# Planning the order of five instruction queues by the longest path, in a linear-attention and MoE kernel

## The chip, the cores and the metric

One core of a Trainium2 chip runs the whole program. The metric is the device time of one execution in microseconds (us). The core's engines are named as in its profile: PE (matrix products), PEld (its weight loads), DVE (vector), ACT (scalar functions), POOL, and SP, which issues the DMAs (its queue is called SPq). Each takes its instructions from a queue of its own, strictly in order.

## The reference

A recurrent linear attention over 768 steps is followed by two MoE layers (one expert each, so plain two-layer networks). Cut to what is computed:

```python
# r, k, v, w, a, b: (4, 8, 768, 40) float32; w_in: (320, 2048), w_out: (2048, 320)
for t in range(S):                                   # for each batch and head
    y[:, :, t] = np.einsum('bhd,bhde->bhe', rt, state)
    Sa = np.einsum('bhde,bhe->bhd', state, at)
    state = state * wt[:, :, None, :] - np.einsum('bhd,bhe->bhde', Sa, bt) + np.einsum('bhd,bhe->bhde', vt, kt)
x = y.transpose(0, 2, 1, 3).reshape(B * S, H * D)    # (3072, 320)
h = x @ moe_w_in;  x = (h * (1.0 / (1.0 + np.exp(-h)))) @ moe_w_out
h = x @ moe2_w_in; out = (h - np.tanh(h)) @ moe2_w_out
```

## The kernel before

The 768 steps are cut into 12 chunks of 64, and the 32 heads into two halves `hf`. Within a chunk the recurrence is a set of matrix products and one triangular solve; from chunk to chunk only the state is carried. A first stage does, chunk by chunk, the attention and the first MoE layer of the chunk's 256 tokens; a second stage then runs the second MoE layer. Large operands are split into a high and a low fp16 plane, so one product takes several matmuls.

The steps of a chunk, with the tile that each writes and the lines of the trace:

- `load_raw`, `prep` (each half): decay products and fp16 planes on DVE, ACT and POOL, written to `HL`; then 12 DMAs of SP copy `HL` into a slot `LR` (L256), and others write `pd`. `load_v` loads `VU`.
- `p1`, `p2`: the first products, `p1a` (L276) and `p1b` (L296). Readers: `mK` on DVE (L284), `bP` on ACT (L289), `KBt` on ACT (L303).
- `sol_in`, 31 `sol_step`s, `sol_out`: the triangular solve for all heads at once, nearly all on DVE: a transpose (L311), then pairs `tmp` and `Tl` (L321, L323), then two transposes (L333, L334). `mrg1`, `mrg2`: products that merge its blocks, tiles `mg` (L342, L356).
- `ch_x`: `psx` (L370, L372) from the carried state `MT`, and `Xs` from it on ACT (L381). `ch_u`: `psu` (L389), read by L398 and L399, and two copies within `LR` (L401). `ch_s`: the scores `pss` (L409) with `psu2` (L410; the trace calls it psu), read into `Sm` on DVE (L418) and `VU` on ACT (L419). `ch_y`: the output `psy` (L428, L431) and the next state `psm` (L442).
- `ch_ye`: the state is scaled into `Md` on DVE (L453), rounded to `MT` on ACT (L455), its low part goes to `lows` on POOL (L196), and two DMAs copy both into `MT` (L457, L458). The next chunk's `ch_x` of this half needs them: this is the recurrence. `ch_m` transposes the state into `M` (L471, L482 to L484).
- `x_t1`, `x_t2`: the output is transposed (`psyt`, L499), scaled (`pf` on DVE, L510) and split into `xh` and `xl`, input of the MoE layer.
- MoE layer 1, eight hidden tiles `i` a chunk: `mm_h` (`hp`, 16 matmuls, L576 and L577), `act1` (Silu, `gh`, `hs` on ACT at L585 to L587, `gl` on POOL), `mm_o` (`o`, 12 matmuls, L600 to L602). Its weights arrive as float64 bits and are converted once, in 32 pieces (`conv_wi`, `conv_wo`; DVE at L531 and L533, the rest on ACT and POOL), into `wih` and `woh`.

PSUM is shared out so: one bank for `hp`, two for `o`, one for `Tl`, and four that all attention tiles take in turn (`ps_a`, `bufs=4`). `gh` and `gl` have three buffers, `hs`, `xh` and `xl` two.

The order is written by hand. A table `SC` gives each step a due time in eighths of a chunk; `when` puts a step no earlier than what it needs, and the tasks run sorted by time:

```python
at(M0 + i, lambda c=c, i=i: mm_h(1, c, i, w1iv, *x_t[c], ps_h))
...
tasks.sort(key=lambda q: (q[0], q[1]))
for t, _, fn, a in tasks:
    fn(*a)
```

The framework (`TileContext` with `schedule_with_timeline_sim=True`) then schedules the instructions on the engines by its own timeline, following the order of the program. The conversions of the first layer are held back by `gates`, four points in chunk 0.

Of the kernel before, what the change touches and what calls it, by code (L numbers as in the profile page):

```python
# [1 line left out]

# [4 lines left out]

F32 = mybir.dt.float32
F16 = mybir.dt.float16
I32 = mybir.dt.int32  # L10
# [37 lines left out]
def _poly():  # L48
# [19 lines left out]
SC = dict(  # L68
    d=(-0.1673, -0.0563, 0.2069),
    r=(0, 0.3799, 0),  # L70
    dm=(-0.1189, -0.1189, -0.1189),
    raw=(-10.4107, -10.4347),
    prep=(-9.6543, -9.4535),
    v=(-4.211, -3.5903),
    p1=(-10.2371, -9.8163, -9.5719, -9.187),
    p2=(1.1248, 2.0285, 1.4012, 1.5709),
# [9 lines left out]
    x=(-0.9631, -0.0175, 2.3021, 1.3623),  # L86
    xe=0.01,
    u=(0.6994, 1.3329, 1.3307, 2.0705),
# [3 lines left out]
    y=(1.4518, 1.9314, 2.2421, 2.7265),  # L92
    ye=0.0248,
    m=(7.3159, 7.953, 8.873, 8.4506),
# [6 lines left out]
    o=3.2447,  # L101
    c1=(-9.2025, 0.5509, 0.821),
# [1 line left out]
)  # L104


def build(tc, pk, tv, w1i, w1o, w2i, w2o, out, nch=NCH, dbg=None):
# [83 lines left out]
    gates = {}  # L191
    y_t, ps_t, x_t, pf_t = {}, {}, {}, {}
    pd = dram.tile([nch, 2, DM, 2, C], F32, name="pd")

# [21 lines left out]
    def prep(c, hf):  # L216
        w, ra, rkb, rrv = raw_t.pop((c, hf))
        hl = HL
        if c == 0 and hf == 1:
            hl = lr_slot().rearrange("p u n -> p (u n)")[0:120, 0:12 * RW].rearrange("p (j n) -> p j n", j=6)  # L220
            DVE.memset(planes(hl)[0][:, :, 3 * C:LW], 0.0)
        ll, rh, lh, rl = planes(hl)
        k0, v0 = (0, 2 * C) if c % 2 == 0 else (C, 0)

        av, kb, rv, vv = [x.rearrange("p (j t) -> p j t", j=6) for x in (ra, rkb, rrv[:, 0:384], rrv[:, 384:768])]

        pt = at_p.tile([120, 392], F32, tag="pq", name="pq", bufs=1)
# [21 lines left out]
        if c == 0:  # L249
            gates["pool"] = nc.cur_bb.bb.instructions[-1]  # L250
# [8 lines left out]
        if c == 0:  # L259
            gates["sp"] = nc.cur_bb.bb.instructions[-1]  # L260
# [57 lines left out]
    def sol_step(c, j):  # L318
        n, w = 31 - j, j // 2 + 1
        tv_ = tmp[:, 0:n * w].rearrange("p (t s) -> p t s", t=n)  # L320
        DVE.tensor_tensor(tv_, Al[:, j + 1:, j:j + 1].to_broadcast([128, n, w]),  # L321
                          Tl[:, j:j + 1, :w].to_broadcast([128, n, w]), ALU.mult)
        DVE.tensor_tensor(Tl[:, j + 1:, :w], Tl[:, j + 1:, :w], tv_, ALU.add)  # L323
        if c == 0:
            gates["dve"] = nc.cur_bb.bb.instructions[-1]

    def sol_out(c):
        bb = 64 * (c % 2)
# [262 lines left out]
    def mm_o(ph, g, i, wo):  # L591
        if i == 0:
            o_t[ph, g] = [ps_o.tile([128, DM], F32, tag=f"o{k}", name=f"o{k}") for k in range(2)]
        gh, gl = g_t.pop((ph, g, i))
        for q in range(2):
            f = 2 * i + q
            for k in range(2):
                cs = slice(256 * q + 128 * k, 256 * q + 128 * k + 128)
                o = o_t[ph, g][k]
                PE.matmul(o, gh[:, cs], wo[f][:, 0], start=f == 0, stop=False)  # L600
                PE.matmul(o, gh[:, cs], wo[f][:, 1], start=False, stop=False)  # L601
                PE.matmul(o, gl[:, cs], wo[f][:, 0], start=False, stop=f == NF - 1)  # L602

    x2d = dram.tile([nch, 2, 2, 128, 384], F16, name="x2d")

# [60 lines left out]
    for c in range(nch):  # L666
# [43 lines left out]
            continue  # L710
        M0 = max(T0 + SC["moe"] + (SC["dm"][c] if c < len(SC["dm"]) else 0), done["x_t2", c, 1] + .001)
        for i in range(8):
            at(M0 + i, lambda c=c, i=i: mm_h(1, c, i, w1iv, *x_t[c], ps_h))
            at(M0 + i + SC["act"], act1, c, i)
            at(M0 + i + SC["o"], mm_o, 1, c, i, w1ov)
        for k in range(2):
            at(M0 + 7 + SC["o"] + .3, out1, c, k)
    if not dbg:
        for f in range(NF):
            at(SC["c1"][0] + f * SC["c1"][1], conv_w1, conv_wi, mo, w1i, wih[:, f], f)  # L720
            at(SC["c1"][0] + SC["c1"][2] + f * SC["c1"][1], conv_w1, conv_wo, mo, w1o, woh[:, f], f)
            for q in range(2):
                n = 2 * f + q
                when(8 * (nch - 1) + SC["c2"][0] + n * SC["c2"][1], conv_w2, f, q, after=[("prep", nch - 1, 1)] + ([("conv_w2", *divmod(n - 1, 2))] if n else []))
    tasks.sort(key=lambda q: (q[0], q[1]))
    for t, _, fn, a in tasks:
        fn(*a)
    ph1.close()
    if not dbg:
        tasks.clear()  # L730
# [13 lines left out]
        for t, _, fn, a in tasks:  # L744
            fn(*a)
    top.close()


def pack(inputs, nch=NCH):
# [28 lines left out]
    return {k: np.ascontiguousarray(v) for k, v in arrays.items()}  # L778


# [14 lines left out]
```

## Time and profile before

| | |
|---|---|
| three runs | 1190.68, 1195.06, 1195.49 us; median 1195.06 |
| profiled execution | 1191.78 us, its span 1190.0 us |
| mean granted clock of PE over the span | 0.924 of full speed |
| busy us in the span: PE, PEld | 930.4 (78%), 754.0 (63%) |
| busy us: DVE, ACT, POOL | 860.6 (72%), 886.4 (74%), 508.7 (43%) |

The span is cut here at 187.5 us, the first Silu of the first hidden tile, and at 862 us, just behind the last Silu of the first layer (858.6). The granted clock is the share of full speed (2.4 GHz) at which PE was let run; a stretch at 0.50 ran at 1.2 GHz. A wait row names the engine and line that waited, and the engine and line whose end released it. "busy" of a group sums the lengths of its instructions; two neighbours on one engine overlap in part, so a matmul of 0.27 us can follow the one before by 0.11.

### The profile page before, as it was taken

What the parts mean: (1) busy time and instruction counts of PE and PEld (TensorE: products, weight loads), DVE (VectorE), ACT (ScalarE), POOL (GpSimd) and SP (SyncE); (2) the same over time, 40 slices, a digit from 0 to 9 for tenths busy, and PEclk for the clock granted to TensorE, in tenths of its full rate; (3) what the DMA queues carried; (4) which work ended last, traced back from release to release, by engine and by line L of the source; (5) the groups of instructions that cost most, each with busy time, mean ns of one, the idle gap of its engine ahead of it and who ended that gap; (6) DMA issues with size and microseconds to landing.
All of it is one profiled execution on the core that took longest, in us unless ns stands there. A gap on an engine that the chain in (4) does not pass through costs nothing.

```text
span 1190.0 us, 32101 instructions
## 1 busy us (share of the span) xinstructions
PE 930.4 (78%) x12624; PEld 754.0 (63%) x12624; DVE 860.6 (72%) x1752; ACT 886.4 (74%) x1718; POOL 508.7 (43%) x550
## 2 busy tenths in 40 slices
PE   0004327878888888897888888888999999999997
PEld 0004326657766666676766766776778888888885
DVE  6677878677877687787778757443188878888885
ACT  2468689757676677576757798998678888888885
POOL 5354564444444454454544334444333333333332
PEclk9999559888889898999889999999989999999999
DMA  6676765444435444445444333344011111111001
GB/s 161 183 199 176 187 171 140 111 118 117 125 99 138 107 119 115 123 113 124 115 108 123 79 105 96 108 124 120 14 27 37 25 26 25 26 31 32 13 12 23
DMA packets 181192, 115.85 MB, mean 97 GB/s; under 512 B 107121, under 2 KB 165553, under 8 KB 181041
## 3 DMA queue, kind: packets, MB, share of 16 engines
q1 hardware_dynamic: 181040, 113.80, 36.5%
q8 instruction: 99, 1.62, 0.6%
q14 instruction: 53, 0.43, 0.1%
HBM read 58.34 MB, written 12.58 MB: 60 GB/s over the span
## 4 chain that ended last, share of the span: by engine, by line
issue 20%; DMA 17%; PE 16%; ACT 15%; DVE 14%; SPq 10%; POOL 9%; POOLq 0%; DVEq 0%; ACTq 0%
POOL gl L196 7%; SPq L256 6%; PE hp L576 6%; DMA LR<-HL 4%; DMA pd<-pq 3%; ACT cr L532 2%; DVE tmp L321 2%; PE o L602 2%; DVE Tl L323 2%; PE o L600 2%; DMA LR<-lows 2%; PE o L601 2%; DVE pq L230 2%; DVE lows L399 2%; DMA x2d<-x2o 1%
## 5 line engine op out<-in xcount | busy, mean ns | idle before, releaser
L576 PE MATMUL hp<-xh,wih 128*128 128x256 f16 x960 | 196.4, 292 | 19.5 <-ACT hs L585 19.5
L196 POOL TENSOR_TENSOR gl<-q,gh 128x512 f16<-128x512 f32 x96 | 111.9, 1167 | 205.6 <-ACT gh L635 205.6
L576 PE MATMUL hp<-x,LR 128*128 128x256 f16 x1344 | 188.7, 274 | 1.9 <-DVE t L633 1.2
L196 POOL TENSOR_TENSOR gl<-hs,gh 128x512 f16<-128x512 f32 x96 | 113.9, 1186 | 150.0 <-ACT hs L587 100.0
L576 PEld LDWEIGHTS <-wih 128*128 128x128 f16 x1344 | 134.1, 104 | 46.2 <-issue 21.2
L576 PEld LDWEIGHTS <-LR 128*128 128x128 f16 x1344 | 132.1, 98 | 25.0 <-issue 2.4
L602 PE MATMUL o<-woh,gl 128*128 128x320 f16 x384 | 113.2, 308 | 8.6 <-POOL gl L196 8.5
L600 PE MATMUL o<-woh,gh 128*128 128x320 f16 x384 | 117.2, 307 | 3.3 <-ACT gh L586 2.1
L601 PE MATMUL o<-woh,gh 128*128 128x320 f16 x384 | 116.6, 306 | 0.0
L600 PE MATMUL o<-LR,gh 128*128 128x320 f16 x384 | 112.9, 302 | 1.3 <-ACT gh L635 1.3
L601 PE MATMUL o<-LR,gh 128*128 128x320 f16 x384 | 113.9, 302 | 0.0
L576 PE MATMUL hp<-xl,wih 128*128 128x256 f16 x384 | 112.2, 292 | 0.0
L321 DVE TENSOR_TENSOR tmp<-Al,Tl 128x126 f32<-128x126 f32 (+22 forms) x372 | 92.5, 249 | 19.2 <-ACT Al L312 10.0
L602 PE MATMUL o<-LR,gl 128*128 128x320 f16 x384 | 104.3, 302 | 0.5 <-POOL gl L196 0.5
L323 DVE TENSOR_TENSOR Tl<-Tl,tmp 128x126 f32<-128x126 f32 (+22 forms) x372 | 95.9, 258 | 9.1
L602 PEld LDWEIGHTS <-gl 128*128 128x128 f16 x768 | 75.4, 99 | 37.5 <-POOL gl L196 12.5
L630 DVE SCALAR_TENSOR_TENSOR s<-s,z 128x512 f32<-128x512 f32 x96 | 74.4, 775 | 33.2 <-ACT s L628 32.2
L600 PEld LDWEIGHTS <-gh 128*128 128x128 f16 x768 | 76.5, 100 | 31.9 <-ACT gh L586 2.7
L632 DVE SCALAR_TENSOR_TENSOR q<-hp,s 128x512 f32<-128x512 f32 x96 | 66.3, 691 | 38.2 <-POOL gl L196 26.2
L601 PEld LDWEIGHTS <-gh 128*128 128x128 f16 x768 | 76.3, 99 | 27.8 <-issue 1.4
L634 DVE COPY_PREDICATED q<-mk,t 128x512 f32<-128x512 int32 x96 | 79.2, 825 | 9.0
L276 PE MATMUL p1a<-LR 120*128 120x64 f16 x384 | 23.3, 211 | 78.6 <-DMA LR<-HL 54.6
(148 smaller groups left out, 2563.3 us busy)
## 6 DMA issues: line engine op xcount, KB each, us to landing
LR<-HL SPq DMA_DIRECT2D x92, 150.9 KB
rawkb<-pk SPq DMA_DIRECT2D x23, 360.0 KB
rawrv<-pk SPq DMA_DIRECT2D x23, 360.0 KB
cr<-w1i SPq DMA_DIRECT2D x16, 384.0 KB
cr<-w2i SPq DMA_DIRECT2D x16, 384.0 KB
cr<-w1o SPq DMA_DIRECT2D x16, 320.0 KB
cr<-w2o SPq DMA_DIRECT2D x16, 320.0 KB
LR<-HL SPq DMA_DIRECT2D x46, 100.6 KB
```

Of the source, the lines that this page charges most:

```text
L196: POOL.tensor_tensor(out, a, b, ALU.subtract)
L230: DVE.tensor_tensor_scan(pt[:, 0:390], w[:, 0:390], d1a.rearrange("p j t -> p (j t)"), 0.0, ALU.mult, ALU.add)
L256: SP.dma_start(out=dst[pl * 40:pl * 40 + 40, :, d0:d0 + w], in_=src[:, :, s0:s0 + w])
L321: DVE.tensor_tensor(tv_, Al[:, j + 1:, j:j + 1].to_broadcast([128, n, w]), Tl[:, j:j + 1, :w].to_broadcast([128, n, w]), ALU.mult)
L323: DVE.tensor_tensor(Tl[:, j + 1:, :w], Tl[:, j + 1:, :w], tv_, ALU.add)
L576: PE.matmul(o, wi[f][:, a], x[:, k], start=n == 0, stop=False)
L600: PE.matmul(o, gh[:, cs], wo[f][:, 0], start=f == 0, stop=False)
L601: PE.matmul(o, gh[:, cs], wo[f][:, 1], start=False, stop=False)
L602: PE.matmul(o, gl[:, cs], wo[f][:, 0], start=False, stop=f == NF - 1)
L630: DVE.scalar_tensor_tensor(out=s, in0=s, scalar=GAMMA, in1=z, op0=ALU.add, op1=ALU.mult)
L632: DVE.scalar_tensor_tensor(out=q, in0=hp, scalar=sh * S_G2, in1=s, op0=ALU.mult, op1=ALU.mult)
L634: DVE.copy_predicated(q, mk.bitcast(I32), t)
```

## The change

`kernel` now builds the program three times. Twice it only traces it: `build` records in `marks` which instructions belong to which task, `units_of` makes units from them (one instruction each on DVE, ACT, POOL and SP; on PE a task's instructions together, hidden products in pieces of 8 and output products in pieces of 6), and `plan` places the units on five engines. It gives each unit a cost (`cost_of`, formulas with constants per engine), a rank (the longest path of costs behind it, with 50000 added for the weight conversions of layer 1) and then repeatedly takes, on the engine that can start first, the unit of the highest rank among those that can start within `LOOK` of it. The four shared PSUM banks are given out in the first trace by when a bank comes free. The first trace yields the order of the tasks, the second the order of the instructions. In the third build the tasks are sorted so, and the instructions of the first stage are chained on each of the five engines by dependencies without a semaphore. The gates are gone. The second stage isn't planned. The mathematics, the tiles and the buffers are the same.

```diff
-    def conv_w1(fn, *a):
-        with ExitStack() as st:
-            for g in gates.values():
-                st.enter_context(tc.issue_after(g))
-            fn(*a)
+    def conv_w1(part, f):
...
-    tasks.sort(key=lambda q: (q[0], q[1]))
+    if order:
+        tasks.sort(key=lambda q: order.get((q[2].__name__,) + q[3], 1 << 30))
+    else:
+        tasks.sort(key=lambda q: (q[0], q[1]))
+    ins = nc.cur_bb.bb.instructions
     for t, _, fn, a in tasks:
+        marks.append((len(ins), fn.__name__, a))
         fn(*a)
...
+HAND = {"PE": 55, "ACT": 35, "DVE": 35, "POOL": 79, "SP": 27}
+DRAIN = {"PE": 0, "ACT": 100, "DVE": 84, "POOL": 40, "SP": -44}
+LOOK = {"PE": 150, "ACT": 60, "DVE": 60, "POOL": 60, "SP": 60}
+BOOST = {"conv_w1": 50000}
+SPLIT = {"h1": 8, "o1": 6}
+SHARED = "a_ps_a"
...
+def latency_of(i, e, cost):
+    if e == "PE":
+        return cost + 170
+    if e == "SP":
+        o = i.outs[0]
+        name = o.bass_ap.tensor.name
+        return 4300 if name[:3] in ("raw", "cr_", "VU_") or name.startswith("LR") and o.ap[0][1] != 40 else 3000
+    return cost
...
+def plan(tc, ins, marks, ordered):
...
+    for n in reversed(order):
+        u = us[n]
+        u.rank = u.late + max([us[m].rank + HAND.get(us[m].e, 0) for m in u.succ], default=0)
...
+                t = max(u.ready, free[e])
+                if e == "PE":
+                    new = [ring_of[x] for x in sorted(u.tiles) if x in ring_of and x not in taken]
+                    if new:
+                        k = live[new[0]] + len(new) - room[new[0]]
+                        if k > len(ends[new[0]]):
+                            continue
+                        if k > 0:
+                            t = max(t, heapq.nsmallest(k, ends[new[0]])[-1])
+                    if u.tiled != tiled:
+                        t += 95
+                c.append((t, n))
...
+        t, n = max((q for q in c if q[0] <= t + LOOK[e]), key=lambda q: (us[q[1]].rank, -q[1]))
...
+    order, _ = traced(None)
+    _, seq = traced(order)
+    nc, args = program()
     with tile.TileContext(nc, schedule_with_timeline_sim=True) as tc:
-        build(tc, aps["pk"], aps["tv"], aps["w1i"], aps["w1o"], aps["w2i"], aps["w2o"], out)
+        build(tc, *args, order=order)
+        ins = list(nc.cur_bb.bb.instructions)
+        info = mybir.DependencyInfo(mybir.DependencyClass.NoSync, mybir.DependencyReason.DATA)
+        for _, v in seq:
+            for x, y in zip(v, v[1:]):
+                tc.add_manual_dep(ins[y], ins[x].name, info, reason="planned order")
```

Three places show what the change does to the built program. The first is DVE in the second half of chunk 0's triangular solve. `tmp` and `Tl` are the solve's steps, `cr` and `c` the two DVE operations of a weight conversion, `mK` reads a first product, `HL` and `pq` belong to `prep`. Before:

```order
L321 TENSOR_TENSOR tmp<-Al,Tl 128x126
L533 SCALAR_TENSOR_TENSOR c_326<-c_326,cr 128x384
L323 TENSOR_TENSOR Tl<-Tl,tmp 128x21x6
L531 TENSOR_SCALAR cr<-cr 128x320
L321 TENSOR_TENSOR tmp<-Al,Tl 128x120
L323 TENSOR_TENSOR Tl<-Tl,tmp 128x20x6
L321 TENSOR_TENSOR tmp<-Al,Tl 128x133
L284 TENSOR_TENSOR mK_122<-p1a,mask_k 64x512
L533 SCALAR_TENSOR_TENSOR c_338<-c_338,cr 128x320
L323 TENSOR_TENSOR Tl<-Tl,tmp 128x19x7
L321 TENSOR_TENSOR tmp<-Al,Tl 128x126
L323 TENSOR_TENSOR Tl<-Tl,tmp 128x18x7
```

After:

```order
L319 TENSOR_TENSOR tmp<-Al,Tl 128x126
L529 SCALAR_TENSOR_TENSOR c_385<-c_385,cr 128x320
L321 TENSOR_TENSOR Tl<-Tl,tmp 128x21x6
L234 TENSOR_SCALAR HL<-pq 120x6
L319 TENSOR_TENSOR tmp<-Al,Tl 128x120
L235 SCALAR_TENSOR_TENSOR HL<-pq,HL 120x6
L321 TENSOR_TENSOR Tl<-Tl,tmp 128x20x6
L319 TENSOR_TENSOR tmp<-Al,Tl 128x133
L321 TENSOR_TENSOR Tl<-Tl,tmp 128x19x7
L319 TENSOR_TENSOR tmp<-Al,Tl 128x126
L321 TENSOR_TENSOR Tl<-Tl,tmp 128x18x7
```

The conversions between the steps are fewer, one operation in this stretch in place of three, and `mK` of the other chunk has gone to a later step.

The second place is PE at the end of that solve. `p1a` are first products (the 6th and 7th tile of the program before, the 8th after), `mg1` and `mg2` the merge of chunk 0, `psu` its U. Before:

```order
L276 LDWEIGHTS LR_676
L276 MATMUL p1a_712<-LR_676 128x64
L342 MATMUL mg1_727<-W1_148,bP_149 32x32 x32
L276 LDWEIGHTS LR_778
L276 MATMUL p1a_797<-LR_778 128x64
```

After:

```order
L274 LDWEIGHTS LR_571
L274 MATMUL p1a_742<-LR_571 128x64
L338 MATMUL mg1_763<-W1_148,bP_149 32x32 x32
L352 MATMUL mg2_806<-TT0_119,W1_148 32x32 x32
L385 MATMUL psu_849<-TT0_119,Xs0_129 40x64
L385 MATMUL psu_849<-TT0_119,Xs1_130 40x64
```

Before, the merge stands ahead of the last two tiles of chunk 1's first products; now it stands behind all eight, and `mg2` and `psu` follow it directly.

The third place is SP in the steady stage, at the copies of the state from chunk 4 to chunk 5, first half (`MT`), among the copies of a prep (`LR<-HL`) and loads of `VU`. Before:

```order
L256 DMA LR<-HL 40x6x322 x2
L256 DMA LR<-HL 40x6x194
L256 DMA LR<-HL 40x6x128
L457 DMA MT<-MT 40x640
L256 DMA LR<-HL 40x6x322
L458 DMA MT<-lows 40x640
L256 DMA LR<-HL 40x6x322
L256 DMA LR<-HL 40x4x194
L256 DMA LR<-HL 40x4x128
L256 DMA LR<-HL 40x4x322
L213 DMA VU_128<-tv 64x640
L256 DMA LR<-HL 40x4x322
```

After:

```order
L256 DMA LR<-HL 40x6x194
L256 DMA LR<-HL 40x6x128
L256 DMA LR<-HL 40x6x322 x2
L256 DMA LR<-HL 40x6x194
L256 DMA LR<-HL 40x6x128
L256 DMA LR<-HL 40x6x322 x2
L256 DMA LR<-HL 40x4x194
L256 DMA LR<-HL 40x4x128
L256 DMA LR<-HL 40x4x322 x2
L453 DMA MT<-MT 40x640
L454 DMA MT<-lows 40x640
L215 DMA VU_127<-tv 64x640
```

The two copies of `MT` stood among the twelve of the prep; now they stand behind all twelve, directly.

## Rows read from the trace of the kernel before

**Rows 1.** Windows by stage: each engine's busy us (x count), granted PE clock, DMA share, GB/s.

```profile
0.00:187.50 187.50, 44.67 (x918) 39.28 (x919) 137.94 (x303) 115.45 (x221) 91.79 (x123) 0.84 0.68 181
187.50:862.00 674.50, 565.87 (x9109) 459.25 (x9110) 458.71 (x1074) 503.29 (x1012) 304.43 (x331) 0.92 0.41 109
862.00:1190.00 328.00, 319.83 (x2600) 255.47 (x2597) 263.97 (x376) 267.64 (x486) 112.46 (x98) 0.98 0.11 25
```

**Rows 2.** Windows around one hole of PE, same columns (PE, PEld, DVE, ACT, POOL).

```profile
283.00:286.40 3.40, 0.07 (x4) 0.07 (x6) 2.45 (x4) 2.51 (x5) 1.88 (x3) 1.00 0.37 113
286.40:293.20 6.80, 6.80 (x100) 5.68 (x101) 6.67 (x7) 6.16 (x12) 4.67 (x5) 0.50 0.39 98
```

**Rows 3.** Waits of PE, 190 to 860 us: total us, times, longest.

```profile
PE hp L576 <- ACT hs L585: 18.8, 17, 4.8
PE pss L409 <- DMA LR<-lows: 11.6, 9, 3.4
PE p1b L296 <- DVE lows L483: 8.7, 6, 3.4
...
PE o L602 <- POOL gl L196: 6.9, 6, 2.1
...
PE psm L442 <- ACT VU L419: 3.2, 4, 2.3
...
PE psy L428 <- DVE Sm L418: 2.8, 4, 1.8
...
PE psx L370 <- ACT bP L289: 1.2, 2, 0.6
```

**Rows 4.** Timeline of PE around 340.6 us: start, length, operation, count.

```profile
340.59 0.27 PE L576 MATMUL hp<-xh,wih 128*128 128x256 f16 x1
340.70 0.27 PE L576 MATMUL hp<-xl,wih 128*128 128x256 f16 x1
```

**Rows 5.** Timelines of PE and ACT around 360 us, one X and its evictions.

```profile
360.01 0.29 PE L372 MATMUL psx<-VU,mK 128*64 128x40 f32 x4
...
360.43 0.88 ACT L381 ACTIVATE Xs<-psx 64x320 f32<-64x320 f32 x2
```

**Rows 6.** Timelines, one Y to the next X; chain of waits (landing); SP's issues.

```profile
735.82 0.23 PE L431 MATMUL psy<-M,LR 120*64 120x40 f16 x2
738.35 0.81 PE L442 MATMUL psm<-VU,KBt 128*40 128x40 f32 x30 [2.30 <-ACT VU L419]
739.80 0.48 DVE L453 SCALAR_TENSOR_TENSOR Md<-psm,p 40x320 f32<-40x320 f32 x1
740.79 0.47 ACT L455 ACTIVATE MT<-Md 40x320 f16<-40x320 f32 x1
742.18 0.81 POOL L196 TENSOR_TENSOR lows<-Md,MT 40x320 f16<-40x320 f32 x1
746.83 0.73 SPq L458 DMA_DIRECT2D MT<-lows  x1
754.76 0.29 PE L372 MATMUL psx<-VU,mK 128*64 128x40 f32 x4
...
284.09 2.03 DMA MT<-lows
...
449.21 4.62 SPq L256 DMA_DIRECT2D LR<-HL  x5
```

**Rows 7.** Timeline of DVE: a conversion inside chunk 0's solve, and three transposes.

```profile
45.46 0.35 DVE L531 TENSOR_SCALAR cr<-cr 128x384 int32<-128x384 int32 x1
45.73 0.55 DVE L533 SCALAR_TENSOR_TENSOR c<-c,cr 128x384 int32<-128x384 int32 x1
...
92.40 1.89 DVE L334 STREAM_TRANSPOSE TT<-Al 64x1024 f32<-64x1024 f32 x1
...
102.65 1.95 DVE L311 STREAM_TRANSPOSE Al<-bP 64x1024 f32<-64x1024 f32 x1
```

**Rows 8.** Timeline of PE: the first merge, with the idle time before it.

```profile
92.64 1.92 PE L342 MATMUL mg<-W,bP 32*32 32x32 f32 x64 [28.27 <-DVE W L333]
```

More of the change, by code (lines that the diff above doesn't have):

```diff
@@ L1 @@
+import heapq
 from contextlib import ExitStack
@@ L4 @@
 import concourse.tile as tile
+import concourse.tile_rust as tile_rust
 from concourse import mybir
@@ L104, with build @@
 )
-def build(tc, pk, tv, w1i, w1o, w2i, w2o, out, nch=NCH, dbg=None):
+def build(tc, pk, tv, w1i, w1o, w2i, w2o, out, nch=NCH, dbg=None, marks=None, order=None):
+    marks = [] if marks is None else marks
     nc = tc.nc
@@ L548, in conv_wo @@
         psub(dst[:, 1], v, dst[:, 0])
-    def conv_w1(fn, *a):
-        with ExitStack() as st:
-            for g in gates.values():
-                st.enter_context(tc.issue_after(g))
-            fn(*a)
+    def conv_w1(part, f):
+        if part == 0:
+            conv_wi(mo, w1i, wih[:, f], f)
+        else:
+            conv_wo(mo, w1o, woh[:, f], f)
     w2 = []
@@ L602, in mm_o, with h1, o1 @@
                 PE.matmul(o, gl[:, cs], wo[f][:, 0], start=False, stop=f == NF - 1)
+    def h1(c, i):
+        mm_h(1, c, i, w1iv, *x_t[c], ps_h)
+    def o1(c, i):
+        mm_o(1, c, i, w1ov)
     x2d = dram.tile([nch, 2, 2, 128, 384], F16, name="x2d")
@@ L712, in build @@
         for i in range(8):
[L713 removed]
+            at(M0 + i, h1, c, i)
             at(M0 + i + SC["act"], act1, c, i)
[L715 removed]
+            at(M0 + i + SC["o"], o1, c, i)
         for k in range(2):
@@ L719, in build @@
         for f in range(NF):
-            at(SC["c1"][0] + f * SC["c1"][1], conv_w1, conv_wi, mo, w1i, wih[:, f], f)
-            at(SC["c1"][0] + SC["c1"][2] + f * SC["c1"][1], conv_w1, conv_wo, mo, w1o, woh[:, f], f)
+            at(SC["c1"][0] + f * SC["c1"][1], conv_w1, 0, f)
+            at(SC["c1"][0] + SC["c1"][2] + f * SC["c1"][1], conv_w1, 1, f)
             for q in range(2):
@@ L746, in build, with size_of @@
     top.close()
+ENGINES = {"EngineType.PE": "PE", "EngineType.Activation": "ACT", "EngineType.DVE": "DVE", "EngineType.Pool": "POOL", "EngineType.SP": "SP"}
+HAND = {"PE": 55, "ACT": 35, "DVE": 35, "POOL": 79, "SP": 27}
[4 more added lines that the diff above has]
+SHARED = "a_ps_a"
+def size_of(x):
+    n = 1
+    for _, c in x.ap[1:]:
+        n *= c
+    return n
@@ new lines, in cost_of @@
+def cost_of(i, e):
+    o = i.outs[0]
+    n, name = size_of(o), o.bass_ap.tensor.name
+    two = sum(hasattr(q, "ap") for q in i.ins) > 1
+    if e == "ACT":
+        return 160 + (2.3 if "int16" in str(o.dtype) else .85) * n
+    if e == "DVE":
+        if i.opcode == "Memset":
+            return 63 + .85 * n
+        if i.opcode == "StreamTranspose":
+            return 140 + 1.72 * n
+        if n in (389, 390):
+            return 960
+        return 150 + 1.05 * n if two else max(170, 60 + .76 * n)
+    if e == "POOL":
+        return 130 + 2.03 * n if two else 60 + 1.05 * n
+    if e == "SP":
+        return 1254 if "Transpose" in i.opcode else 780 if name.startswith("LR") and o.ap[0][1] == 40 else 440
+    m = o.ap[0][1]
+    if "float32" in str(i.ins[0].dtype):
+        return 109 if m == 128 else {(40, 64): 56, (64, 40): 58, (40, 40): 38, (32, 32): 31}[m, n]
+    return max(27, n * .425) if m == 128 or n >= 128 else {64: 19}.get(m, 13)
@@ new lines, in latency_of, with units_of @@
+def latency_of(i, e, cost):
+    if e == "PE":
+        return cost + 170
+    if e == "SP":
+        o = i.outs[0]
+        name = o.bass_ap.tensor.name
+        return 4300 if name[:3] in ("raw", "cr_", "VU_") or name.startswith("LR") and o.ap[0][1] != 40 else 3000
+    return cost
+class Unit:
+    __slots__ = ("e", "ins", "cost", "late", "succ", "pred", "rank", "ready", "name", "args", "tiles", "tiled", "two", "left", "hold", "holds", "start")
+def units_of(tc, ins, marks):
+    at = {i.name: k for k, i in enumerate(ins)}
+    n1 = marks[-1][0]
+    task = [(-1, "init", ())] * n1
+    for (a, nm, ar), (b, _, _) in zip(marks, marks[1:]):
+        task[a:b] = [(a, nm, ar)] * (b - a)
+    us, of, cur = [], [], {}
+    for k in range(n1):
+        i = ins[k]
+        e = ENGINES.get(str(i.engine))
+        if not i.outs or not hasattr(i.outs[0], "ap"):
+            e = None
+        t = task[k]
+        u = cur.get(t[0]) if e == "PE" else None
+        if u is None or len(us[u].ins) >= SPLIT.get(t[1], 999):
+            u = len(us)
+            v = Unit()
+            v.e, v.ins, v.cost, v.late, v.succ, v.name, v.args = e, [], 0, 0, set(), t[1], t[2]
+            v.tiles, v.tiled, v.two = set(), False, False
+            us.append(v)
+            if e == "PE":
+                cur = {t[0]: u}
+        of.append(u)
+        v = us[u]
+        v.ins.append(k)
+        if e:
+            c = cost_of(i, e)
+            v.cost += c
+            v.late = latency_of(i, e, v.cost)
+            v.two = e == "DVE" and sum(hasattr(q, "ap") and "PSUM" not in str(q.bass_ap.space) for q in i.ins) > 1
+            v.tiled = e == "PE" and tuple(i.tile_size or (128, 128)) != (128, 128)
+        v.tiles |= {t.name for t in tile_rust.get_accessed_tiles(i, tc.info.uid)}
+    for k in range(n1):
+        for d in ins[k].descendants or ():
+            d = at[d]
+            if d < n1 and of[d] != of[k]:
+                us[of[k]].succ.add(of[d])
+    return us
@@ new lines, in order_of @@
+def order_of(us):
+    key = [(u.name,) + u.args for u in us]
+    when, left, after = {}, {}, {}
+    for n, u in enumerate(us):
+        k = key[n]
+        if u.e:
+            when[k] = min(when.get(k, (u.start, n)), (u.start, n))
+        left.setdefault(k, 0)
+        after.setdefault(k, set()).update(key[m] for m in u.succ if key[m] != k)
+    for v in after.values():
+        for k in v:
+            left[k] += 1
+    todo = [(when.get(k, (0, 0)), k) for k, c in left.items() if not c]
+    heapq.heapify(todo)
+    order = {}
+    while todo:
+        _, k = heapq.heappop(todo)
+        order[k] = len(order)
+        for m in sorted(after[k], key=str):
+            left[m] -= 1
+            if not left[m]:
+                heapq.heappush(todo, (when.get(m, (0, 0)), m))
+    assert len(order) == len(left)
+    return order
@@ L778, in pack @@
     return {k: np.ascontiguousarray(v) for k, v in arrays.items()}
+class Traced(Exception):
+    pass
 def kernel(**inputs):
```

169 lines of the change are left out of this document (157 added, 12 removed).

## The prediction, made before the changed kernel was run

> **What bounds the kernel now.** I read the stages first [rows 1]: to 187.5 us (the first hidden layer's first Silu) the tensor engine is busy 44.67 us, from there to 862 it is busy 565.87 of 674.5 us, and in the second MoE layer 319.83 of 328. That last stage is full and its code is untouched, so what the change can win lies ahead of 862. In the middle stage PE is idle 674.5 - 565.87 = 108.6 us, and no other engine is full: DVE 458.71 and ACT 503.29 of 674.5. Next I read the clock. Just ahead of 286.40 PE was busy for 0.07 of 3.4 us; then it ran 6.80 us without a gap at a granted clock of 0.50, which is the lower of its two levels (1.2 against 2.4 GHz) [rows 2]. So a hole costs twice: the hole, and work at half speed behind it. Over the middle stage the granted clock is 0.92 [rows 1]: (1 - 0.92) x 674.5 = 54 us of full speed are missing, some 49 us of them under work, since PE is busy about nine tenths of the slow stretches.
>
> Then the waits of PE in 190 to 860 us [rows 3]. They are small and of three kinds. A hidden-layer product waits for the Silu that frees its only PSUM bank (18.8 us in 17 waits). Attention products wait for a reader of an earlier tile to free one of the four shared PSUM banks: nine such rows, 8.7 down to 1.2 us, together 36.3. Products wait for data just made: the score products 11.6, the output layer 6.9 for POOL, the state and output products of attention 3.2 and 2.8 for VU and Sm. The rest is spread over small rows, and some 15 us have none. Nothing here is a full engine; it is the order in five queues, which is what the change replaces.
>
> **The change, part by part.** Instructions, tiles and buffers are the same in number and size; all that is priced is order. For the order of PE I measure distance in PE work between two rows at full speed, with the spacing of rows in the trace: 0.11 us for a hidden product [rows 4], and in the same way 0.14 for an output one and 0.02 to 0.06 for the small ones.
>
> PSUM banks. The plan decides at each step which tile takes the next of the four banks, by when one comes free, and keeps the rest waiting while hidden and output products, cut into halves, run. The 36.3 us go; between 0 and 36 of them could come back as other waits, and I take the row's full value, pricing the new waits below. -36.
>
> Hidden to hidden. Of 95 steps from one hidden tile to the next, 12 now have at most 0.5 us of PE work between them. Each wait in the old row is 18.8/17 = 1.1 us, so these cost 12 x 0.9 = 11 in place of 18.8. -8.
>
> Output, Sm and VU. From hidden tile to its low-half output product the distance grows from a mean of 10.6 to 14.7 us, from the score products to the output products of attention from 0.3 to 8.2 us. Of 6.9 + 3.2 + 2.8 I leave 2. -11.
>
> X to U. Here the cover shrinks, from a mean of 6.8 us to 2.4; five of 22 have only 0.4. X's last products start at 360.01 and last 0.29, its two evictions end at 361.31: 1.0 us [rows 5]. 5 x 0.6 = 3. If the evictions stand behind other ACT work at twice that, 14. +3. Scores keep their 11.6: the cover from U to S is 9.5 before and 10.3 now.
>
> Y to the next X. This is the recurrence, and here the order got tighter. The PE work between Y and the next chunk's X was 15.8 to 22.4 us and is now 7.0 to 17.3 in the 17 places of the steady stage. What must happen in between is, at the least, 0.81 us of state products, twice 0.48 + 0.47 + 0.81 on DVE, ACT and POOL, 0.73 of issue and 2.03 of landing, 7.1 us together; the shortest that the trace has is 736.05 to 754.76, 18.7 [rows 6]. Neither end is near this order, so I take the middle, 12.9. With PE work stretched to elapsed time at a busy share of 0.9 the 17 covers miss it by 22 us in all; at 7.1 they miss nothing, at 18.7 some 101. +22.
>
> Sum of the idle time: 108.6 - 36 - 8 - 11 + 3 + 22 = 79, which is 30 less. The clock follows the holes [rows 2]: 49 x 30/108.6 = 13 less; its ends are 0 and 49 us. The Trainium skill, TensorE: Matmul & The Clock Gate, Part 1, puts the penalty of the ramp under 1% of a typical kernel span, to be left out of a model. By that it is at most 12 us here and 3 of them would go, for a forecast of 1146; the row with 0.92 speaks against it.
>
> The first 187.5 us. Between the 62 steps of chunk 0's solve stood 11 of the weight conversions; now 5. A conversion is 0.35 + 0.55 us on DVE [rows 7], so 6 x 0.9 = 5.4 us leave the solve. Two tiles of chunk 1's first products stood behind the merge, which PE reached after a hole of 28.27 us [rows 8]; now all stand ahead of it. Chunk 1's solve, whose first transpose starts at 102.65, can then start when chunk 0's last one ends, at 94.29 [rows 7], 8.4 us sooner. Against that DVE has 5 us more work ahead of the last piece of the first hidden input (138 us against 133, summed with the durations of before); at its share of 0.74 that is 6.8. -5.4 - 8.4 + 6.8 = -7; the ends are +7, if only the last counts, and -30, if most of DVE's 49.6 idle us close. PE has 25 us of work behind it at that point in place of 19. -6.
>
> The other side of this: only 17 of 32 first-layer conversions stand ahead of that point on DVE, where 27 stood, and the last comes beside the solve of chunk 4. Chunk 0's hidden products wait for them; what covers is the attention of chunks 2 and 3, and if it doesn't, PE idles there as it does now. In the last stage the conversions of the second layer and the first 20 Square rows stand at the same amount of ACT work in both orders, so nothing is priced there.
>
> Sum: 1191.78 - 30 - 13 - 7 - 6 = 1136. It stands on the profiled execution, which lies inside the three runs (1190.68 to 1195.49, median 1195.06), so I don't shift it.
>
> **Rivals.** Slower: the copies that carry the recurrence wait on SP. In 9 of 22 places the two MT copies now stand directly behind all 12 copies of a prep, where at most 5 stood. Five take 4.62 us to issue [rows 6], 12 take 11.1; 7.1 + 11.1 = 18.2, in effect the slowest end above. Idle time is then 79 - 22 + 101 = 158, which is 49 more than now, the clock loses 22 more, the start still wins 13: 1250. It decides from where Y to X takes 16 us: the misses are then 61 and gain and loss cancel. For it: the order itself, and POOL and ACT must finish the prep before the 12 can go. Against it: the plan books SP's time and places the copies where it expects the data later than the burst.
>
> No change: the freed bank waits return one for one, because the readers that free the banks stand in DVE's and ACT's queues, which are still in fixed order; the 36 come back, with the clock's share 52, which leaves 1136 + 52 = 1188. For it: nothing in a plan makes a reader faster. Against it: DVE has 32% idle time in the middle stage and ACT 25% [rows 1], and hidden and output products are there to run in between.
>
> Much faster: Y to X takes 7 to 9 us, the 15 us without a row close too, idle falls to 45 and the clock stays up (-64 - 29), and the start gains 20: 1079. For it: attention now runs about one chunk ahead, so hidden products are there to fill holes. Against: a start like that would need DVE 0.9 busy; it is at 0.74, with DMA at 0.68 [rows 1].
>
> That the plan is not followed I leave out: the built order shows the moves.
>
> **How the numbers follow.** Forecast 1136, chance 0.57, with a range of its own from 1090 (Y to X free of misses and the start at its better end) to 1186 (misses of 55). Much faster, below 1090: 0.13. No change: 0.10. Slower: 0.20. The range for 8 in 10 leaves out the outer half of each end: 1075 to 1215. A measurement of this kernel can tell about 0.5%, 6 us, from no change. Faster 0.57 + 0.13 = 0.70, same 0.10, slower 0.20.
>
> **What would show it.** Right: in the middle stage PE busy near 0.88 and a granted clock of 0.94 or more, the rows of PE behind readers of PSUM (the p1a, p1b and psx rows) below 10 us together, and the second layer unchanged at 328. Wrong in the recurrence: psx or the psm that shares its input waiting for MT's copies by tens of us, with SP issuing LR copies ahead of them. Wrong at the start: first Silu later than 187.5, with hidden products waiting for POOL's wih. The forecast falls altogether if the second layer's stretch grows, which no step here allows for.

## The result and the profile after

The changed kernel takes 1130.38 us (1124.21 to 1134.49, four runs) against 1195.21 before: a ratio of 0.946, 95% interval 0.941 to 0.951. 1136 was forecast. The profiled execution took 1129.98 us, its span 1128.3. Cut like [rows 1], at the first Silu (165.7) and just behind the last one of the first layer (803.5), and with the middle stage cut once more at the end of chunk 0's eighth Silu (270.9), the windows of the changed kernel are (engines in the order PE, PEld, DVE, ACT, POOL, then granted clock, DMA share, GB/s):

```profile
0.00:165.70 165.70, 50.70 (x1000) 44.79 (x1001) 131.72 (x310) 97.56 (x189) 73.29 (x104) 0.80 0.64 168
165.70:270.90 105.20, 76.08 (x1315) 60.39 (x1315) 88.44 (x213) 83.93 (x170) 52.97 (x58) 0.76 0.63 161
270.90:803.50 532.60, 480.78 (x7706) 393.23 (x7706) 363.59 (x855) 434.52 (x874) 264.96 (x291) 0.96 0.45 118
165.70:803.50 637.80, 556.86 (x9021) 453.62 (x9021) 452.03 (x1067) 518.45 (x1042) 317.93 (x349) 0.92 0.48 125
803.50:1128.30 324.80, 316.51 (x2605) 254.06 (x2602) 263.75 (x376) 267.82 (x487) 112.97 (x99) 1.00 0.11 26
```

The first Silu comes 21.8 us earlier, the middle stage is 36.7 shorter (idle 108.6 to 80.9, busy 565.87 to 556.86), the last 3.2. That is all of the 61.7 us between the spans. The second line is the new weak place: chunk 0's hidden tiles take 105.2 us, where they took 53.2, and PE idles 29.1 of them at a clock of 0.76. Behind it the granted clock is 0.96.

The waits of PE in 165 to 803 us (total us, times, longest), to be read beside [rows 3]:

```profile
PE hp L572 <- ACT hs L581: 30.0, 32, 2.1
PE hp L572 <- ACT wih L535: 7.8, 3, 4.1
PE pss L405 <- DVE lows L395: 4.8, 1, 4.8
PE p1b L294 <- ACT y L458: 4.5, 6, 1.0
...
PE psyt L495 <- DVE lows L479: 2.7, 1, 2.7
PE psx L368 <- DMA VU<-tv: 2.4, 3, 1.4
PE o L598 <- POOL gl L198: 2.4, 3, 1.6
PE psu L385 <- ACT Xs L377: 2.1, 5, 0.8
...
PE pss L405 <- DMA LR<-lows: 0.5, 1, 0.5
```

Attention products that wait until the reader of another attention tile gives its PSUM bank back do so for 24.7 us, all such rows together, where it was 45.5 before. (The prediction's nine rows, 36.3, leave out psu behind `lows`, 5.6, and the smallest ones.) The largest now is one wait of pss behind `lows`, 4.8 us; it is for a bank, since pss starts at 200.62, 0.06 us behind the end of that `lows` and ahead of the issue of its copy at 200.88. The scores' wait for their copies, 11.6 before, and those for VU and Sm are nearly gone, and that of the output products for POOL fell from 6.9 to 2.4. The wait of a hidden product for its Silu grew from 18.8 to 30.0 us, in short pieces. There is no row in which psx waits for the copies of MT.

At the start the solves of the first two chunks got short. Windows over chunk 0's and chunk 1's solve, first before, then after (the third engine is DVE):

```profile
44.00:87.80 43.80, 1.33 (x16) 0.94 (x16) 34.24 (x96) 25.99 (x49) 24.07 (x29) 1.00 0.72 192
107.70:161.10 53.40, 15.98 (x291) 14.54 (x290) 42.93 (x112) 37.06 (x77) 29.87 (x35) 0.61 0.66 177
```

```profile
46.10:77.80 31.70, 1.97 (x28) 1.57 (x28) 28.89 (x86) 15.73 (x30) 17.41 (x20) 1.00 0.64 169
93.00:130.00 37.00, 8.98 (x147) 7.53 (x147) 34.26 (x97) 20.15 (x44) 18.63 (x22) 0.53 0.59 155
```

Of the 12.1 us that chunk 0's solve lost, 5.4 are work of DVE and 6.7 its idle time (9.6 to 2.8). The waits of DVE over both solves (44 to 161 us before, 46 to 130 after) say for what:

```profile
DVE cr L531 <- ACT c L530: 7.3, 8, 2.0
DVE HL L232 <- DMA LR<-HL: 4.7, 2, 3.3
DVE c L533 <- ACT cr L532: 4.2, 11, 0.7
```

```profile
DVE W L329 <- ACT Al L326: 1.6, 1, 1.6
...
DVE cr L527 <- ACT c L526: 1.1, 3, 0.7
DVE HL L234 <- DMA LR<-HL: 1.1, 1, 1.1
```

A conversion is a relay of ACT and DVE. Put between two solve steps, it made the solve wait for ACT as well: 11.5 us before (6.1 of them in chunk 0's solve, 4.2 in chunk 1's), 1.1 after. It need not do so. Between the steps of the two solves stood 21 and 21 of the conversions' DVE operations before and stand 9 and 9 after; in c4 below they are 13 and 17, and yet DVE idles only 2.0 and 1.9 us there. The windows of these two solves in c4:

```profile
51.10:86.70 35.60, 2.28 (x28) 1.70 (x28) 33.58 (x91) 20.24 (x37) 19.21 (x22) 1.00 0.68 174
97.50:140.90 43.40, 11.79 (x192) 9.79 (x187) 41.55 (x107) 29.25 (x58) 24.08 (x28) 1.00 0.65 167
```

### The profile page after: what moved, and what is told of

Read it like the earlier page. It is cut to its first block, busy times and chain, and to the rows that moved or that the text cites. A ratio compares the mean times of both kernels' runs of the same rounds, so it can differ in the third digit from the quotient of the medians.

```text
span 1128.3 us, 32086 instructions
## 1 busy us (share of the span) xinstructions
PE 924.1 (82%) x12624; PEld 752.5 (67%) x12624; DVE 847.5 (75%) x1752; ACT 883.8 (78%) x1718; POOL 504.2 (45%) x550
## 5 line engine op out<-in xcount | busy, mean ns | idle before, releaser
L572 PE MATMUL hp<-xh,wih 128*128 128x256 f16 x960 | 186.7, 283 | 39.7 <-ACT hs L581 30.0
L572 PEld LDWEIGHTS <-wih 128*128 128x128 f16 x1344 | 130.7, 100 | 70.1 <-issue 36.4
L572 PEld LDWEIGHTS <-LR 128*128 128x128 f16 x1344 | 131.4, 98 | 24.7 <-issue 2.5
L598 PE MATMUL o<-woh,gl 128*128 128x320 f16 x384 | 116.4, 303 | 2.4 <-POOL gl L198 2.4
L596 PE MATMUL o<-LR,gh 128*128 128x320 f16 x384 | 111.6, 299 | 1.4 <-ACT gh L637 1.3
L597 PE MATMUL o<-LR,gh 128*128 128x320 f16 x384 | 112.7, 299 | 0.0
L572 PE MATMUL hp<-xl,wih 128*128 128x256 f16 x384 | 108.5, 283 | 0.0
```

## The experiments

All times are medians of four runs beside runs of the kernel before on the same chip (c3: ten). Experiments that change the plan carry one more rule in it. It is there because with other numbers the plan could put a use of a later LR slot ahead of that slot's turn, and the queues would wait for each other in a circle; no run here shows that case:

```diff
-                if users[x][0] != users[y][0]:
-                    us[users[x][0]].succ.add(users[y][0])
+                us[users[x][0]].succ.update(q for q in users[y] if q != users[x][0])
```

**c1, the rule alone.**

> The plan gets one more rule: in a ring of buffers every user of a later tile, not only its first, comes after the first user of the tile ahead of it. The planned order changes in places and nothing else. If the gain of the change (1130.38 us, ratio 0.9462) is a property of planning and not of one lucky order: 1122 to 1140. If single orders scatter by more than that, the experiments that change one number of the plan can be read only for differences above that scatter.

1129.75 us, ratio 0.951 (0.946 to 0.955): a second planned order gives the same, so the gain is not that of one lucky order. It is the reference for c3 to c5.

**c2, task order without the chains.**

```diff
-        for _, v in seq:
+        for _, v in []:
```

> The tasks are sorted in the planned order, but the instructions are not chained on the engines; the framework's own scheduler issues them. Theory A (the gain lies in the order of single instructions: halves of hidden products between attention steps on PE, few foreign operations in a solve on DVE): most of the gain goes, 1170 to 1200. Theory B (the order of tasks, which sets who takes the next buffer, is what counts): 1130 to 1145.

1203.28 us, ratio 1.012 (1.007 to 1.017). The whole gain is gone, and a little more: theory A, 3 us above its range. The window from the first Silu (198.6) to the end of the first layer:

```profile
198.60:874.90 676.30, 560.47 (x8976) 449.64 (x8976) 446.13 (x1023) 497.17 (x992) 297.40 (x324) 0.93 0.41 109
```

PE idles 115.8 us in the middle stage, and the start is 33 us longer than with the chains.

**c6 and c7, the chain on PE alone, and on the other four alone.**

```diff
-        for _, v in seq:
+        for e, v in seq:
+            if e != "PE":        # c7: if e == "PE"
+                continue
```

> The changed kernel with the chain on PE alone; DVE, ACT, POOL and SP are ordered by the framework's scheduler. With no chain at all 1203.28 was measured. Theory A (the gain is PE's order: hidden and output products in between attention steps): 1135 to 1155. Theory B (the gain is that readers and copies on the other four queues come in the planned order, so that PE's order meets its data): 1185 to 1215.

> The counterpart: DVE, ACT, POOL and SP are chained as planned, PE is ordered by the framework's scheduler. Theory A (the gain is PE's order): 1175 to 1205. Theory B (the gain is the order of the other four): 1135 to 1160. If this one and the run with PE's chain alone both stay near 1203, the gain needs both.

1249.92 and 1220.02 us. Each is slower than no chain at all (1203.28; by the ratios 1.048 and 1.022 against 1.012, where the intervals of c7 and c2 just touch). So neither theory holds in its simple form, and the last sentence of the second text comes closest: the gain needs both, and one half is worse than none. First the window of c6 behind its first Silu (201.3), then both of c7:

```profile
201.30:924.00 722.70, 587.66 (x9022) 473.06 (x9021) 443.44 (x1012) 497.50 (x990) 298.97 (x323) 0.87 0.38 102
```

```profile
0.00:162.80 162.80, 51.65 (x1000) 45.85 (x1000) 132.06 (x308) 96.92 (x189) 72.00 (x104) 1.00 0.65 171
162.80:894.10 731.30, 604.90 (x9024) 466.51 (x9024) 454.13 (x1069) 518.56 (x1044) 309.67 (x349) 0.89 0.41 109
```

The start is decided by the other four queues: with them in planned order the first Silu comes at 162.8, without at 201.3. The middle stage needs PE's order to fit theirs. With PE's chain alone, hidden products wait 67.1 us for Silu in 33 waits; with PE free and the rest fixed, p1a waits 22.4 us for LR copies.

**c3 and c4, weight conversions late and early.**

```diff
-BOOST = {"conv_w1": 50000}
+BOOST = {"conv_w1": 0}        # c4: 150000
```

> The weight conversions of the first layer lose their 50000 of rank (and the ring rule of the control is in). Theory A (chunk 0's hidden products stand in PE's queue waiting for converted weights, 105.2 us from its first Silu to the last in place of 53 before, and that costs time at the end): the second chunk's first Silu comes 30 to 60 us later than 274.6 and the total is 1150 to 1190. Theory B (attention of later chunks runs ahead meanwhile, so the work is only exchanged): 1125 to 1140, with attention further ahead.

> The weight conversions get 150000 of rank in place of 50000 (and the ring rule of the control is in), so they stand ahead of nearly all attention work in the first 160 us. Theory A (hidden products of chunk 0 wait for weights): the stretch from its first to its last Silu falls from 105.2 to 60 to 80 us and the total to 1105 to 1122. Theory B (DVE's work ahead of the first solve sets the start, so conversions between solve steps delay all that follows): first Silu later than 170 and a total of 1130 to 1150.

1180.00 us (ratio 0.992) and 1117.53 us (0.940, 0.935 to 0.945): theory A in both, by the total. Two signs of c4 came out otherwise: the stretch fell to 46.4 us, further than the 60 to 80 of theory A, and the first Silu, at 177.1, is later than 170, as theory B had it. In c3 the second chunk's first Silu comes at 333.0, 58 us later than after. The stretch of chunk 0's hidden tiles in c3, and PE's wait rows there:

```profile
154.80:329.40 174.60, 105.81 (x1427) 73.42 (x1427) 120.09 (x288) 118.09 (x229) 66.29 (x79) 0.56 0.51 137
```

```profile
PE hp L572 <- ACT wih L535: 13.2, 9, 4.2
...
PE o L596 <- ACT woh L543: 6.8, 5, 1.9
```

With the two rows of POOL's halves (5.0), waits for weights are 25.0 of the 68.8 us that PE idles in this stretch. The rest stands in other rows, and whether those are what late weights leave behind isn't shown. That stretch in c4, then its whole middle stage:

```profile
177.10:223.50 46.40, 36.93 (x653) 29.68 (x652) 39.01 (x93) 41.93 (x81) 24.88 (x25) 0.93 0.56 137
177.10:794.20 617.10, 539.74 (x9031) 442.25 (x9030) 445.17 (x1057) 501.08 (x1002) 301.77 (x332) 0.95 0.46 122
```

In c4 the stretch is 46.4 us in place of 105.2 and the total falls by only 12. The span shows where the rest stayed: the first Silu is 11.4 us later, the idle time of the middle stage is nearly the same (77.4), and PE's busy time there is 17.1 us less. (Against c1, its reference, the first Silu is 15.0 us later, the idle time 8.3 less and the busy time 14.3 less.) What early conversions give is mostly the clock.

**c5, tasks in the hand's order, instructions planned.**

```diff
-    order, _ = traced(None)
+    order = None
     _, seq = traced(order)
...
-                us, seq = plan(tc, list(nc.cur_bb.bb.instructions), marks, order is not None)
+                us, seq = plan(tc, list(nc.cur_bb.bb.instructions), marks, True)
```

> The tasks stay in the order written by hand, which also sets who takes the next buffer, the four shared PSUM banks among them; the plan only orders and chains the instructions on the five engines within that (ring rule of the control in, gates gone). Theory A (as the prediction has it, 36 us of waits go because the plan gives the banks out by the time that one comes free): most of that comes back with the clock's share, 1160 to 1180. Theory B (the order of single instructions is the gain, and with it bank waits go whoever takes the bank): 1125 to 1140.

1148.51 us, ratio 0.964 (0.959 to 0.969), between the theories. By the ratios, ordering the instructions within the hand's turns of the buffers gives 3.6%; the planned turns bring it to 4.9% (c1).

**c9, only the banks in the hand's turn**, on top of c4:

```diff
-    order, _ = traced(None)
+    order, _ = traced(None, True)      # plan(..., ordered=True) in the first trace too
```

> As the run with early conversions (1117.53), but the four shared PSUM banks go round in the order written by hand in both traces, instead of going to the tile that the first trace puts next; task order, splitting and chains are planned as before. Theory A (the prediction's largest term: 36 us of bank waits go because of this): at least 20 us more, 1138 to 1160, with p1a, p1b and psyt waiting for readers. Theory B (the order of single instructions removes those waits in either turn): 1112 to 1126.

1140.90 us, ratio 0.959 (0.955 to 0.963), 23 us above c4: theory A in size, without its sign. p1a and p1b hardly wait (3.0 us in the largest row), and all waits for banks are 25.6 us against 16.6 in c4. A product that may not have its bank yet doesn't wait in PE's queue; the plan puts it later. From the last state product (psm) to the next X, 18 steady places add up to 530 us in place of 296 in c4, read from the timelines of PE. But that this pace costs the time isn't shown: the same sum is 595 us in c5, which takes 1148.51, and 457 in the kernel before, which takes 1195.21. The largest row that is new is

```profile
PE o L598 <- POOL gl L198: 10.9, 8, 3.2
```

and where the rest of the 23 us lies stays open.

**c8, the state's copies pushed back.**

```diff
+            for q in range(4 if extra is not None else 0):
+                extra.append(len(nc.cur_bb.bb.instructions))
+                SP.dma_start(out=spare[c, hf, q], in_=MT[0:40].rearrange("p u j n -> p (u j n)"))
             SP.dma_start(out=MT[40:80], in_=MT[0:40])
```

> The changed kernel, same order, with four more DMAs on SP directly ahead of each of the 22 pairs of copies that carry the state (each writes the high plane of MT to a spare place in DRAM; nothing reads it). At 0.76 us of issue each they push the copies back by 3 us. In the trace of after, from the landing of the second copy (taken as 2.03 us behind its issue) to the next chunk's X it is less than 3 us in 15 of 22 places, and the shortfalls add up to 29 us. Theory A (X stands just behind the copies, so the recurrence sets the pace): 29 us more and the clock's share, 1159 to 1172. Theory B (hidden products cover the recurrence with room, as the lack of any wait of psx for MT in the trace says): 1128 to 1140.

1152.30 us, ratio 0.966 (0.963 to 0.970), between the ranges of the two theories. The four copies took 1.4 to 2.9 us, in most places 1.6, and not 3.0. SP's timeline shows one place, with two of PE's wait rows behind it:

```profile
297.75 1.60 SPq L456 DMA_DIRECT2D spare<-MT  x4
299.46 0.78 SPq L457 DMA_DIRECT2D MT<-MT  x1
```

```profile
PE psx L367 <- DMA MT<-lows: 6.6, 4, 2.4
PE psm L471 <- DMA MT<-lows: 6.2, 4, 2.7
```

So 22 x 1.6 = 35 us of pushing cost 22 us, and 12.8 us of waits for MT stand where none of psx for MT had stood: the copies have little room, as in theory A. How much of the 22 us is the recurrence is open. The delay also stands ahead of the VU loads, whose row at psx rose from 2.4 to 8.3 us; the two can't be told apart here. And the slack says less. The shortest time from a second copy's issue to X in c8 is 2.15 us; by that, 1.6 us are missing in 8 of the 22 places of after, 5 us together. Nor is the loss even: at the same products of PE, c8 is at most 6 us behind after up to 490 us, with 13 pushes past, and 18 us behind at 644, with six more.

**c10, whole tasks on PE** (on c4):

```diff
-SPLIT = {"h1": 8, "o1": 6}
+SPLIT = {"h1": 999, "o1": 999}
```

> As the run with early conversions (1117.53), but a task's hidden and output products are one unit on PE (16 and 12 matmuls in a row) instead of pieces of 8 and 6. Theory A (pieces fill PE's holes and free attention steps from standing behind a whole tile, 1.8 us at full speed): 1128 to 1145. Theory B (the holes are longer than a tile or not there): 1112 to 1124.

1119.51 us, ratio 0.940 (0.936 to 0.944), the same as c4: theory B. Halves are not what made the gain.

**c11, a second bank for hp, three for attention** (on c4):

```diff
-    ps_h = top.enter_context(tc.tile_pool(name="ps_h", bufs=1, space=PSUM))
+    ps_h = top.enter_context(tc.tile_pool(name="ps_h", bufs=2, space=PSUM))
...
-    ps_a = ph1.enter_context(tc.tile_pool(name="ps_a", bufs=4, space=PSUM))
+    ps_a = ph1.enter_context(tc.tile_pool(name="ps_a", bufs=3, space=PSUM))
```

> As the run with early conversions (1117.53), but hp has two PSUM banks and the attention tiles three in place of four; the plan knows both numbers. There, hidden products wait 31.7 us in 30 places for the Silu that frees the only hp bank. Theory A (those waits are on the path): most of the 31.7 go, and three attention banks cost little since the plan orders around them, 1090 to 1108. Theory B (PE waits there because nothing else is ready, and the wait moves to another row, or three banks cost as much): 1112 to 1135.

1123.57 us, ratio 0.944 (0.940 to 0.948): no gain. The row that it aimed at did go, from 31.7 us in c4 to

```profile
PE hp L572 <- ACT hs L581: 6.4, 6, 3.0
```

yet the idle time of the middle stage fell only from 77.4 to 69.8 us, and the profiled span is 1118.6 us against 1119.0. Attention, with one bank less, waits 30.1 us for banks in place of 16.6, and PE's busy time over the span grew from 908.3 to 915.6 us. So taking the largest wait row away took no time away here: theory B. Which of its two reasons holds, a wait that only moves or a third bank that costs as much, this run can't tell.

**c12, another plan**: output products whole, more rank for the conversions.

```diff
-BOOST = {"conv_w1": 50000}
-SPLIT = {"h1": 8, "o1": 6}
+BOOST = {"conv_w1": 300000}
+SPLIT = {"h1": 8, "o1": 12}
```

> As the run with early conversions (1117.53), with output products whole (pieces of 12, hidden ones still of 8) and 300000 of rank for the conversions. The plan's own clock ends 15 us earlier for it than for the early-conversion kernel. Theory A (the plan's order of merit holds on the chip): 1100 to 1112. Theory B (differences of 2% between plans are below what its costs know of the chip): 1112 to 1130.

1099.68 us (1098.54 to 1100.92), ratio 0.924 (0.920 to 0.927): the best of all, 31 us below the changed kernel, and theory A. Which of the two numbers did it isn't separated. Its window from the first Silu (178.5) to the end of the first layer:

```profile
178.50:772.40 593.90, 531.45 (x9029) 435.49 (x9029) 441.16 (x1057) 499.37 (x1004) 305.37 (x333) 0.97 0.47 126
```

The middle stage idles 62.5 us at a clock of 0.97. The end that the plan itself computes for the first stage (us) ranks these nine fully chained kernels in the order of their medians, though it knows no clock. Some neighbours are closer than the noise, and by the ratios c1 (0.951) and after (0.946) change places:

```
kernel      c12     c4     c10    c11    c1    after    c9     c5     c3
plan's end  668    683     684    687    695    698    700    708    757
median   1099.7 1117.5  1119.5 1123.6 1129.8 1130.4 1140.9 1148.5 1180.0
```

## Why the prediction came out right, and where its steps did not

The sum was nearly exact, and two of its five parts were. That it came out is in part luck: the clock gave 10 us less than forecast, and the start gave 15 more. From the two spans, in the prediction's terms:

| part | forecast | measured |
|---|---|---|
| idle time of PE in the middle stage | -30 | 108.6 to 80.9: -27.7 |
| work that PE does before the first Silu | -6 | 44.67 to 50.70: -6.0 |
| the clock in the middle stage | -13 | busy -9.0, less the 6.0 moved: -3.0 |
| first Silu | -7 | 187.5 to 165.7: -21.8 |
| second layer | 0 | 328.0 to 324.8: -3.2 |

**Idle time.** Inside this part the terms shifted. Banks gave 45.5 - 24.7 = 21 us of rows, not 36 (the p1a, p1b and psx rows among them are 5.7, below the 10 that were to show the step right); output, Sm and VU gave 10 of the forecast 11; scores, which were to keep their 11.6, lost most of it; X to U gave nothing instead of costing 3. Hidden to hidden was to win 8 and lost 11.2, and Y to X was to cost 22 in rows of psx and shows none. These last two, 11 + 22 = 33 in the forecast against 30.0 in the Silu row, may be one thing: the plan fills the time until MT lands with hidden products and takes X the moment it expects the copies, so what the cover lacks would show as a hidden product's wait for Silu. The trace doesn't show that it is so. In the 18 steady places from psm to the next X, 265.5 us long in all, lie 46.0 of the 80.9 us of idle time, 25.3 of them ahead of hidden products; but only 15.9 of these are waits for Silu, and 7.8 are waits for converted weights. In the kernel before the same places, 457 us long, held 68 us of idle time. c8 shows that the copies at their end have little room. The "15 us without a row" of the prediction was a misreading: the rows of 190 to 860 us add up to 106 of the 108.6.

**The rival "slower"** had its mechanism right: copies of MT do wait behind the burst of a prep. In eight of the nine places with all twelve ahead, the second copy is issued 3.5 to 7.0 us after `lows` is ready. One place, on SP, with POOL's end of `lows` ahead of it and PE's X behind it:

```profile
290.40 0.79 POOL L198 TENSOR_TENSOR lows<-Md,MT 40x320 f16<-40x320 f32 x1 [1.00 <-ACT MT L451]
```

```profile
285.29 9.98 SPq L256 DMA_DIRECT2D LR<-HL  x12
295.38 0.76 SPq L453 DMA_DIRECT2D MT<-MT  x1
296.25 0.74 SPq L454 DMA_DIRECT2D MT<-lows  x1
```

```profile
298.75 0.40 PE L274 MATMUL p1a<-LR 120*128 120x64 f16 x8
299.08 0.38 PE L467 MATMUL psm<-istk,MT 120*40 120x40 f16 x16
299.30 0.19 PE L366 MATMUL psx<-MT,LR 120*64 120x40 f16 x2
```

`lows` is ready at 291.19 and its copy is issued at 296.25; X starts at 299.30 with PE busy up to it. Its price was wrong. At this place 5.9 of the burst's 10 us pass before `lows` is ready, so the copy is 5.1 us late and not 11.1. From the end of Y to X it takes 15.9 us in the mean of the 18 places (26.1 before): not the rival's 18.2, but also not the 12.9 of the sum, and close to the 16 from which gain and loss were to cancel. They did not cancel, so the reckoning of the misses was too dear.

**No change** (the bank waits return one for one) is refuted by the rows, and c9 prices the planned turns at 23 us. Only 9 of these are waits for banks; that such turns are worth more than the waits that they remove, the prediction didn't see.

**The clock** is the step that failed. The remark "if it doesn't, PE idles there as it does now" gave the late conversions no price. PE's idle time during chunk 0's hidden tiles went from 11.5 to 29.1 us and the clock there to 0.76. At that clock (1 - 0.76) x 105.2 = 25 us of full speed are missing in the stretch, where it was (1 - 0.92) x 53.2 = 4; by the busy share of 76.08 in 105.2, an estimate, some 18 of the 25 lie under work, in place of 3. This took back most of the 13; the 0.94 that was to show the step right is 0.92, and only behind that stretch 0.96. c3 and c4 bear this out: the same matmuls (9021 of them) are busy 582.49 us in c3 and 556.86 in after; c4, with 9031, has 539.74. The Trainium skill, TensorE: Matmul & The Clock Gate, Part 1, puts the ramp under 1% of a typical kernel span. The prediction took that as a bound on all that the clock costs, and as such this trace doesn't bear it out: (1 - 0.92) x 637.8 = 51 us of full speed are missing in the middle stage of after alone, some 45 of them under work by its busy share, 3.9% of the span. The 3.0 us that the clock gave are just what the prediction drew from that rule, but not for its reason: a loss in one stretch met a gain in the others. Between orders of the same work the rows differ by far more, 582.49 - 539.74 = 42.8 us from c3 to c4, 3.8% of the span of after.

**The start** was taken at -7 between +7 and -30, and came out at -21.8, near the better end. Up to chunk 0's second `pf`, DVE's last step of the first hidden input, 11.9 us were won (it ends at 170.50 before and 158.65 after), and up to POOL's `xl` behind it 13.9 (174.42 and 160.46). The windows up to that `pf`, before and after:

```profile
0.00:170.50 170.50, 33.43 (x662) 29.77 (x663) 124.24 (x276) 100.33 (x193) 81.52 (x114) 0.85 0.66 176
```

```profile
0.00:158.60 158.60, 45.63 (x895) 40.17 (x896) 125.74 (x291) 91.84 (x178) 69.83 (x99) 0.80 0.65 169
```

DVE's work there rose by 1.5 us, where the sum had 5, and its idle time fell by 13.4 (46.3 to 32.9). The failed term is the 5.4 us for conversions that leave the solve. They left it (5.4 us of work less), but other work took their place ahead of `pf`. What was won is idle time, which the sum kept at DVE's old share of 0.74; the share rose to 0.79. DVE's waits for ACT's half of a conversion fell by 6.5 us there (11.5 to 5.0), and mK's for p1a by 5.3 (12.4 to 7.1).

The other 7.9 us lie behind `xl`, in PE's order, and no term of the sum had them. Before, PE began the first hidden tile, stood ahead of a merge and of p1b, and went on with the tile at 180.90; after, the tile starts 0.7 us behind `xl`:

```profile
173.21 0.39 PE L576 MATMUL hp<-xh,wih 128*128 128x256 f16 x1
...
180.35 0.72 PE L296 MATMUL p1b<-istk,LR 120*128 120x40 f16 x16 [3.71 <-DVE lows L483]
180.90 0.38 PE L576 MATMUL hp<-xl,wih 128*128 128x256 f16 x1
```

```profile
161.12 0.27 PE L572 MATMUL hp<-xh,wih 128*128 128x256 f16 x1
```

## What to carry to other kernels

An order is worth something only if all queues keep it: five chains gave 5.4%, PE's chain alone or the other four alone cost more than none. Where a queue relays work with another engine, price a foreign instruction in a serial section with the wait for its partner, not with its own length alone; c4 shows that an order can avoid that wait. And when PE's order is planned tightly, a wait row names where it ran out of fill, not what it would gain without the wait: in c11 the largest row went and the time stayed, and in c8 a delay where no row stood cost 22 us.

## What the runs showed of the hardware

The mean granted clock of a span says little of the time. Runs of the kernel before lasted 1190.41 us at 0.920 and 1190.60 at 0.958, and 1182.85 at 0.925 and 1182.33 at 0.958. Where the difference lies in these runs no trace tells. One place where it can lie is the start, where PE has some 50 us of work in 165: after had 0.80 there, c7, with the same order on the four other queues, 1.00, and the first Silu came at 165.7 and 162.8. A clock tells more of a stretch in which PE has much to do, as the 0.56 in c3, where PE was busy for 105.8 of 174.6 us. And a DMA's issue on SP took 0.40 us when it wrote 40 rows to one place in DRAM, where it was 0.76 for the copies of MT within SBUF; that made c8's push half of what was meant.
